# Strided q and k transposes issued one pair step earlier, and the attention of chunk 1 begun with its first layer-1 block

## The chip, the cores and the metric

The kernel runs on one core of one Trainium2 chip. The metric is the device time of one execution in microseconds (us). Engines are named as in the profile: PE (TensorE matmul), PEld (its weight loads), DVE (VectorE), ACT (ScalarE), POOL (GpSimd) and SP (SyncE, which here only issues DMAs).

## The reference, cut to what matters

Sparse attention over 8 batches, 8 heads, 576 positions and head size 64, followed by a two-layer network over the 4608 tokens.

```python
mask_local = (rel >= 0) & (rel < stride)                                    # heads 0-3, stride 32
mask_strided = (rel >= 0) & (pos[None, :] % stride == pos[:, None] % stride)  # heads 4-7
...
attn = exp(masked scores); attn = attn / sum; out = attn @ v
x = attn_out.transpose(0, 2, 1, 3).reshape(B * S, H * D)     # 4608 x 512
h = x @ w_in                                                 # 512 -> 2048
g = np.maximum(h, 0.0) + alpha * np.minimum(h, 0.0)
return g @ w_out                                             # 2048 -> 512
```

## The kernel before, in words

**Chunks.** The network works on nine chunks of 512 tokens. For each chunk, sixteen layer-1 blocks (`lin1_piece`, four matmuls at L636, then a negative part on ACT at L646 and the combination into `gT` on DVE at L649) are followed by layer 2: sixteen pieces of plain matmuls in chunks 0 and 1 (L663), and fourteen blocks of a scheme with sums of quadrants in the later chunks (`lin2_sums`, matmuls at L759, sums at L705).

**Attention between the blocks.** The attention of later batches is cut into small pieces in one list, and after each block of the network some of them run. A pair `g` is two heads of one batch: `g // 4` is the batch, `g % 4` of 0 and 1 are local pairs, 2 and 3 strided ones. The list is made by "pair steps" `g`: in step `g`, the scores of pair `g` (piece S, `score_both`, matmuls L411, exponentials L424 and L430 on ACT, masks L426 and L433 on POOL), the products with v of pair `g - 1` (pieces P, `pv_piece`, L454, then L461 and L463 on DVE), and in some steps the TensorE transposes of a local q and k (pieces T and Tk, L251). A piece also issues loads and casts.

**Order of chunk 1.** The loop from L923 on spreads the pieces of a chunk evenly with an accumulator: `left` pieces over the blocks, half a share per layer-1 block. In chunk 1, `skip = 4` leaves the first four layer-1 blocks without attention and makes the share of the others larger.

**Strided q and k of batches 2 to 7.** `load_d` (L133) loads both into `qks` (names `qsd`, `ksd`) by two DMAs of the POOL queue; for batch c + 1 it is called in step `4c + 2`, for batch 2 ahead of the loop. `transpose_d` (L140) then issues two transposing DMAs from SP, into `qTs[1]` and `kTs[1]`. It is called in the last P piece of step `4c` for batch c. The first reader is the S piece of step `4c + 2` (scores of pairs 10, 14, 18, 22, 26, 30, here called S10 to S30). The last earlier reader of the same tiles is the S piece of step `4c - 1`.

**SP in order.** SP issues, in the order of the program, the stores of the output (L669 and L712), the loads of local q and k (L126), the transposes of attention results (`x_dma`: `xs<-x16s` at L486 for the first strided pair of a batch, `xT<-x` at L488 for local pairs) and `transpose_d`. In step `4c + 3` the last P piece calls `x_dma` for pair `4c + 2`; that is L486. The tile `xs` is read by an ACT copy at L493 (`x_copy`) two steps later.

Of the kernel before, what the change touches and what calls it, by code (L numbers as in the profile page):

```python
# [31 lines left out]
def kernel(  # L32
# [13 lines left out]
    B, H, S, D = q.shape  # L46
# [52 lines left out]
    DX = 2  # L99
# [12 lines left out]
    def load_qk(b, strided, nm):  # L112

        h0 = 4 if strided else 0
        src = q if nm == "q" else k
        if strided and b:
            t16 = hpool.tile([128, 2, 512], F16, tag=f"{nm}s", bufs=2, name=f"{nm}s")
            cast16[(b, True, nm)] = t16  # L120
        else:
            t16 = hpool.tile([128, 2, 512], F32, tag=f"{nm}l", bufs=2, name=f"{nm}l")
            loaded[(b, strided, nm)] = t16
        base = src[b, h0 : h0 + 1, 0:1, :]
        eng = nc.sync if (b > 2 and not strided) or (b == 0 and strided) else nc.gpsimd
        keep(eng.dma_start(t16, bass.AP(  # L126
            tensor=base.tensor, offset=base.offset,
            ap=[[8 * D, 64], [2 * S * D, 2], [S * D, 2], [1, 8 * D]])))
# [7 lines left out]
    def transpose_d():  # L136

        for nm, dst in (("q", qTs[1]), ("k", kTs[1])):
            o = dst.rearrange("r e c -> r (e c)")[:, 0:1280].rearrange("r (j p) -> r j p", p=80)
            keep(nc.sync.dma_start_transpose(o, qks[nm].rearrange("p h c -> p (h c)")))  # L140
# [10 lines left out]
    def cast_l(b, nm, eng="pool"):  # L151
        t16 = hpool.tile([128, 8, 2, 64], F16, tag=f"{nm}l16", bufs=2, name=f"{nm}l16")
        cast_copy(eng, t16, loaded[(b, False, nm)].rearrange("p f (t d) -> p t f d", t=8))
        cast16[(b, False, nm)] = t16

    def load_tail(b, strided):

        t16 = tpool.tile([128, 512], F16, tag="tl", name="tl16")
        for i, src in enumerate((q, k)):
            if strided:  # L160
                keep(nc.gpsimd.dma_start(
                    t16[32 * i : 32 * i + 32, :].rearrange("x (h c) -> x h c", h=4),
                    src[b, 4:8, 512:576, :].rearrange("h (x c) d -> x h (c d)", c=2)))
            else:
                keep(nc.gpsimd.dma_start(
                    t16[64 * i : 64 * i + 64, 0:256].rearrange("p (h d) -> p h d", h=4),
                    src[b, 0:4, 512:576, :].rearrange("h p d -> p h d")))
        cast16[(b, strided, "tail")] = t16

    def load_v(b, strided):  # L170


        if strided:
            st = spool.tile([128, 2048], F16, tag="v", bufs=2, name="stv")
            keep(nc.gpsimd.dma_start(
                st[0:72, :].rearrange("p (h e) -> p h e", h=4),
                v[b, 4:8, :, :].rearrange("h (p t) d -> p h (t d)", t=8)))
            loaded[b] = st
        else:
            v16 = vls[b % 2]  # L180
            base = v[b, 0:1, 0:1, :]
            r0 = 32 if b < 2 else 0
            keep(nc.gpsimd.dma_start(
                v16[r0:128, :, 0:64],
                bass.AP(tensor=base.tensor, offset=base.offset - (32 - r0) * D,
                        ap=[[D, 128 - r0], [96 * D, 24], [1, D]])))
            cast16[(b, False, "v")] = v16
# [9 lines left out]
    def cast_v(b, pr, eng):  # L197

        v16 = vss[b % 2]
        cast_copy(eng, v16[0:72, 2 * pr : 2 * pr + 2, :, 0:64],  # L200
                  loaded[b][0:72, 1024 * pr : 1024 * pr + 1024].rearrange(
                      "p (h t d) -> p h t d", h=2, t=8))
        cast16[(b, True, "v")] = v16
# [300 lines left out]
    def T(u, nm):  # L504
        return lambda: transpose_piece(u, nm)
# [4 lines left out]
    def Pv(g, i):  # L510
        return lambda: pv_piece(pairs[g], i)

    def X(g):
        return lambda: x_piece(pairs[g])
# [27 lines left out]
    for g in range(7, npair + 2):  # L542
        c = g // 4
        a, p, t = g, g - 1, g + 1
        okA = 8 <= a < npair
        okP = 8 <= p < npair
        okT = 8 <= t < npair and (t % 4 == 0 or t < 4 * DX and t % 2 == 0)
        nP = len(pairs[p].pgroups) if okP else 0
        seq = []
        if okA:  # L550
            seq.append(("S", lambda a=a: score_both(pairs[a])))
        if okP:
            seq.append(("P", Pv(p, 0)))
        if okT:
            seq.append(("T", T(t // 2, "q")))
        if 8 <= g - 2 < npair and not pairs[g - 2].xd:
            seq.append(("X", X(g - 2)))
        if okP:
            seq.append(("P", Pv(p, 1)))
        if okT:  # L560
            seq.append(("Tk", T(t // 2, "k")))
        if nP == 3:
            seq.append(("P", Pv(p, 2)))
        if not seq:
            seq.append(("N", lambda: None))

        todo = [(c, pr) for pr in range(2)] if g % 4 == 0 and 8 <= g < npair else []

        if g % 4 == 1 and 9 <= g and c + 1 < B:
            todo = [(c + 1, nm) for nm in "qk"]  # L570
        lastP = max([i for i, z in enumerate(seq) if z[0] == "P"], default=len(seq) - 1)
        nslots = [i for i, z in enumerate(seq) if z[0][0] != "S"] or list(range(len(seq)))
        for i, (kind, fn) in enumerate(seq):
            extra = []
            if todo and i in nslots:
                left = len([z for z in nslots if z >= i])
                cnt = -(-len(todo) // max(1, left))
                extra = [todo.pop(0) for _ in range(min(cnt, len(todo)))]

            def run(fn=fn, extra=extra, g=g, c=c, kind=kind, lastp=(i == lastP), first=(i == 0)):  # L580
                fn()
                for b, pr in extra:
                    if pr in ("q", "k"):
                        cast_l(b, pr)
                        if b + 1 < B:
                            load_qk(b + 1, False, pr)
                        continue
                    cast_v(b, pr, "pool")
                    if pr == 1 and b + 1 < B:
                        load_v(b + 1, True)  # L590
                if kind == "Tk" and g % 4 == 3 and c + 3 < B:
                    load_tail(c + 3, False)
                if lastp:
                    if 4 * DX <= g - 1 < npair and pairs[g - 1].xd:
                        x_dma(pairs[g - 1])
                    if g % 4 == 0 and DX <= c < B:
                        transpose_d()
                    if g % 4 == 2 and DX <= c and c + 1 < B:
                        load_d(c + 1)
                    if g % 4 == 1 and DX < c and c + 1 < B:  # L600
                        load_v(c + 1, False)
                if first and 4 * DX <= g - 3 < npair and pairs[g - 3].xd and pairs[g - 3].strided:
                    x_copy(pairs[g - 3])
            feed(run, g - 2 if kind == "X" else -1)
# [318 lines left out]
    for n in range(1, NCH):  # L923
        ab = attn_until(n + 1) if n + 1 < B else len(pieces)
        left = ab - pos["i"]
        skip = 4 if n == 1 else 0
        acc = 0.0
        for i in range(32 if n == 1 else 30):
            if i < 16:
                if quiet(n):  # L930
                    lin1_piece(n, 8 * (i % 2) + i // 2)
                    if i in (3, 7, 11):
                        late.append(lambda i=i: g_sum(nc.gpsimd, n, 1, i // 2 - 1, i // 2 + 1))
                else:
                    lin1_piece(n, i)
                    if n > 1 and i in (10, 12):
                        g_sum(nc.gpsimd, n, 3, 2 * i - 20, 2 * i - 16)
                    if n > 1 and i == 13:
                        late.append(lambda: g_sum(nc.vector, n, 1, 0, 4))
            elif n == 1:  # L940
                lin2_piece(n, i - 16)
            else:
                lin2_sums(n, i - 16)
                if n == 2 and i == 20:
                    w_sums(nc.vector, (3,))
            if i >= skip:
                acc += left / ((22.5 if n == 1 else 19 if n == B - 2 else 20.5) - 0.5 * skip) * (0.5 if i < 16 else 1.0)
            cnt = int(acc)
            acc -= cnt
            attn_n(cnt, ab)  # L950
        while pos["i"] < ab:
            attn_step(ab)
# [30 lines left out]
```

The softmax here doesn't subtract the row's maximum and nothing guards it: scores larger than these inputs give would overflow.

## Time and profile before

| what | value |
|---|---|
| median of 5 runs | 324.2 us |
| the 5 runs | 323.23, 323.28, 325.19, 324.2, 328.4 us |
| the profiled execution | 323.23 us, of which 321.5 us are the span |
| PE busy | 303.1 us (94% of the span) |
| DVE, ACT, POOL busy | 221.3, 180.7, 171.8 us |
| software DMA queue (q0, from POOL), hardware queue (q1, from SP) | 49.6% and 33.4% of 16 engines' span |

The span runs from the first to the last instruction of the program; 1.7 us of the execution's time lie outside it. Busy shares are averages over stages: layers 1 and 2 of chunks 1 to 5 with attention between them (66 to 232 us) have other limits than the last chunks, in which no attention is left. A wait in the profile is named by the engine that waits, its line, and what released it.

### The profile page before, as it was taken

The numbers are of one execution on the slowest core, as the hardware profiler recorded it, in microseconds if no ns is written. First come the engines' busy times: TensorE is split into PE (matmuls) and PEld (weight loads), VectorE is DVE, ScalarE is ACT, GpSimd is POOL, SyncE is SP. The second block draws the span as 40 slices with busy tenths as digits, with TensorE's granted clock in tenths as the row PEclk, the third lists the DMA queues.
The fourth block names the chain that finished last, engine by engine and source line by source line (L and its number), as shares of the span: only waits on it lengthen the run. The fifth ranks groups of instructions, "written<-read, shape, count | busy, mean of one in ns | idle before, by whom it ended". The sixth has DMA issues, their size and how long they took to land.

```text
span 321.5 us, 7079 instructions
## 1 busy us (share of the span) xinstructions
PE 303.1 (94%) x2813; PEld 194.6 (61%) x2813; DVE 221.3 (69%) x403; ACT 180.7 (56%) x331; POOL 171.8 (53%) x170
## 2 busy tenths in 40 slices
PE   7699989999999999999998999799999999999995
PEld 2365446554454457745787878346864794585484
DVE  5466855766633789578756895578658986865872
ACT  1565655459566666477556745576477527624730
POOL 8672397323999691969195908494536501200300
PEclk9999999999999999999999999999999999999999
DMA  7999999999389991999369935993281122002003
GB/s 217 191 205 206 225 177 167 183 207 240 64 152 144 247 120 9 116 272 155 37 99 226 198 38 97 139 154 45 48 187 20 19 83 70 2 33 100 0 2 132
DMA packets 81057, 40.38 MB, mean 126 GB/s; under 512 B 58480, under 2 KB 76160, under 8 KB 81024
## 3 DMA queue, kind: packets, MB, share of 16 engines
q0 software_dynamic: 41728, 17.38, 49.6%
q1 hardware_dynamic: 39296, 22.55, 33.4%
q8 instruction: 22, 0.36, 0.5%
q14 instruction: 11, 0.09, 0.1%
HBM read 38.01 MB, written 9.44 MB: 148 GB/s over the span
## 4 chain that ended last, share of the span: by engine, by line
PE 63%; DMA 12%; DVE 12%; ACT 6%; issue 3%; POOL 2%; SPq 1%; ACTq 0%
PE hb L636 22%; PE hb L759 21%; DMA kT<-ksd 10%; PE hb L663 7%; DVE gT L649 6%; PE pv L454 3%; DMA kl<-in_k_dram 2%; DVE gsum L705 2%; DVE x L463 2%; ACT neg L646 2%; PE sp L411 2%; PE tp L251 2%; PE hb L817 2%; PE opl L759 1%; ACT et L430 1%
## 5 line engine op out<-in xcount | busy, mean ns | idle before, releaser
L649 DVE SCALAR_TENSOR_TENSOR gT<-neg,oma,hb 128x512 f16<-128x512 f32 x144 | 105.3, 744 | 43.7 <-ACT neg L646 36.7
L636 PE MATMUL hb<-xT,win 128*128 128x512 f16 (+1 forms) x640 | 132.6, 358 | 0.7
L646 ACT ACTIVATE neg<-hb 128x512 f32<-128x512 f32 x144 | 86.1, 598 | 39.1 <-PE hb L636 37.6
L636 PEld LDWEIGHTS <-win 128*128 128x128 f16 x640 | 60.2, 98 | 56.8 <-issue 2.7
L426 POOL TENSOR_TENSOR et<-et,consts 128x576 f16<-128x576 f16 (+1 forms) x24 | 30.6, 1274 | 64.6 <-ACT et L424 64.3
L705 POOL TENSOR_TENSOR gsum<-gT 128x1024 f16<-128x1024 f16 (+1 forms) x16 | 28.0, 1766 | 42.2 <-DVE gT L649 42.2
L759 PEld LDWEIGHTS <-gsum 128*128 128x128 f16 x448 | 41.8, 98 | 5.0
L759 PEld LDWEIGHTS <-gT 128*128 128x128 f16 x336 | 31.4, 98 | 8.4 <-issue 3.4
L463 DVE TENSOR_TENSOR x<-pv,rc 96x384 f16<-96x384 f32 (+2 forms) x62 | 33.0, 532 | 2.1
L663 PE MATMUL hb<-wout,gT 128*128 128x512 f16 x128 | 32.7, 379 | 0.1
L461 DVE RECIPROCAL rc<-pv 72x6 f32<-72x6 f32 (+2 forms) x80 | 14.7, 183 | 25.2 <-PE pv L454 24.9
L433 POOL TENSOR_TENSOR et<-et,consts 128x576 f16<-128x576 f16 (+1 forms) x24 | 30.9, 1288 | 0.9 <-ACT et L430 0.6
L454 PEld LDWEIGHTS <-et 72*128 72x128 f16 (+1 forms) x448 | 24.1, 98 | 10.8 <-POOL et L433 0.9
L759 PE MATMUL hb<-wout,gT 128*128 128x256 f16 x216 | 27.4, 273 | 3.0 <-DVE gT L649 3.0
L771 ACT COPY o<-hb 128x512 f32<-128x512 f32 (+1 forms) x28 | 15.8, 564 | 24.5 <-PE hb L759 24.2
L424 ACT ACTIVATE et<-sp 128x576 f16<-128x576 f32 (+1 forms) x24 | 15.5, 646 | 21.8 <-PE sp L411 21.8
L759 PE MATMUL hb<-wsum,gsum 128*128 128x256 f16 x216 | 26.3, 273 | 0.0
L759 PE MATMUL hb<-wout,gsum 128*128 128x256 f16 x216 | 26.2, 272 | 0.0
L774 DVE TENSOR_TENSOR o<-hb,o 128x512 f32<-128x512 f32 (+1 forms) x21 | 14.2, 678 | 12.7 <-PE hb L759 8.7
L430 ACT ACTIVATE et<-sph 128x288 f16<-128x288 f32 (+1 forms) x48 | 18.5, 407 | 0.0
L817 PE MATMUL hb<-gsum 128*128 128x512 f16 x44 | 16.4, 449 | 1.2 <-DVE gsum L829 1.2
L663 PEld LDWEIGHTS <-gT 128*128 128x128 f16 x128 | 10.7, 97 | 8.7 <-issue 0.2
(107 smaller groups left out, 328.6 us busy)
## 6 DMA issues: line engine op xcount, KB each, us to landing
out_dram<-o SPq DMA_DIRECT2D x27, 256.0 KB, 2.5
ql<-in_q_dram SPq DMA_DIRECT2D x6, 512.0 KB, 5.3
kl<-in_k_dram SPq DMA_DIRECT2D x6, 512.0 KB, 6.6
stv<-in_v_dram POOLq DMA_DIRECT2D x8, 288.0 KB, 7.9
vl<-in_v_dram POOLq DMA_DIRECT2D x6, 384.0 KB, 12.2
win<-in_moe_w_in_dram POOLq DMA_DIRECT2D x4, 512.0 KB, 9.6
wout<-in_moe_w_out_dram POOLq DMA_DIRECT2D x4, 512.0 KB, 13.2
out_dram<-osb SPq DMA_DIRECT2D x8, 256.0 KB, 3.9
```

The costliest lines, as they stand in the source:

```text
L426: keep(nc.gpsimd.tensor_tensor(mv, mv, m, op=ALU.mult))
L430: keep(nc.scalar.activation(ev[:, n * y : n * y + n], sps[y][0:r, 0:n], AF.Exp, scale=SCALE))
L433: keep(nc.gpsimd.tensor_tensor(mv, mv, m, op=ALU.mult))
L454: keep(nc.tensor.matmul(pv[:, 65 * x : 65 * x + 65], et[0:r, c : c + 128], v16[0:r, 2 * P.pr + hh, t, :] if P.strided else v16[:, 6 * (2 * ...
L463: keep(nc.vector.tensor_tensor(P.x16[0:w, c0 : c0 + 64 * nb].rearrange("r (c e) -> r c e", e=64), pvv[:, :, 0:64], rc[0:w, 0:nb].unsqueeze ...
L636: keep(nc.tensor.matmul(hps[:, dst : dst + w], win16[:, kk, 128 * m : 128 * m + 128], xT[:, kk, src : src + w], start=(kk == 0 and x == 0) ...
L646: keep(nc.scalar.activation(neg, hps, AF.Relu, scale=-1.0))
L649: keep(nc.vector.scalar_tensor_tensor(gTs[n][:, m, :], neg, oma[:, m : m + 1], hps, op0=ALU.mult, op1=ALU.add))
L663: keep(nc.tensor.matmul(ops, gTs[n][:, kf, 128 * mt : 128 * mt + 128], wout16[:, kf, :], start=(kf == 0), stop=(kf == 15)))
L705: keep(eng.tensor_tensor(o[:, k0:k1], x[:, k0:k1], y[:, k0:k1], op=op))
L759: keep(nc.tensor.matmul(dst, lhs[:, kf, 128 * mt : 128 * mt + 128], rhs[:, kf, :], start=(first and own and kf == 0), stop=(kf == 7), skip ...
L817: keep(nc.tensor.matmul(wps, wrm[:, 0:128], wrm, start=True, stop=True))
```

## The change

`transpose_d()` is called in the last P piece of step `4c + 3` for batch c + 1, right behind `x_dma`, instead of in step `4c + 4`. For batch 2 it moves from the S piece of step 8 to the Tk piece of step 7. In chunk 1 the accumulator starts with the first layer-1 block, and the divisor is the 22.5 that was there without the skip.

```diff
@@ -593,7 +593,7 @@
                 if lastp:
                     if 4 * DX <= g - 1 < npair and pairs[g - 1].xd:
                         x_dma(pairs[g - 1])
-                    if g % 4 == 0 and DX <= c < B:
+                    if g % 4 == 3 and DX <= c + 1 < B:
                         transpose_d()
                     if g % 4 == 2 and DX <= c and c + 1 < B:
                         load_d(c + 1)
@@ -923,7 +923,6 @@
     for n in range(1, NCH):
         ab = attn_until(n + 1) if n + 1 < B else len(pieces)
         left = ab - pos["i"]
-        skip = 4 if n == 1 else 0
         acc = 0.0
         for i in range(32 if n == 1 else 30):
             if i < 16:
@@ -943,8 +942,7 @@
                 lin2_sums(n, i - 16)
                 if n == 2 and i == 20:
                     w_sums(nc.vector, (3,))
-            if i >= skip:
-                acc += left / ((22.5 if n == 1 else 19 if n == B - 2 else 20.5) - 0.5 * skip) * (0.5 if i < 16 else 1.0)
+            acc += left / (22.5 if n == 1 else 19 if n == B - 2 else 20.5) * (0.5 if i < 16 else 1.0)
             cnt = int(acc)
             acc -= cnt
             attn_n(cnt, ab)
```

## The prediction

> **What bounds the kernel now.** I read the page's slices first, then PE's waits, the timeline at each of those waits, SP's timeline ahead of them, and last the landing times of the transfers. The slices of the page (40 of 8.04 us) show PE nearly full, at full clock:
>
> ```profile
> PE   7699989999999999999998999799999999999995
> PEclk9999999999999999999999999999999999999999
> ```
>
> So a microsecond in which PE stands still is a microsecond of the span, unless another engine takes it back later. PE's two largest waits after the start-up (us in total, times, longest):
>
> ```profile
> PE sp L411 <- DMA kT<-ksd: 3.7, 3, 2.1
> PE hb L759 <- DVE gT L649: 3.0, 4, 0.8
> ```
>
> The first is what the change aims at. The timeline shows where it lies (start, us, instruction; in brackets PE's idle time before it):
>
> ```profile
> 107.47 0.30 PE L411 MATMUL sp<-qT,kT 64*128 64x72 f16 x8 [0.70 <-DMA kT<-ksd]
> ...
> 140.29 0.30 PE L411 MATMUL sp<-qT,kT 64*128 64x72 f16 x8
> ...
> 173.70 0.30 PE L411 MATMUL sp<-qT,kT 64*128 64x72 f16 x8 [0.82 <-DMA kT<-ksd]
> ...
> 208.36 0.30 PE L411 MATMUL sp<-qT,kT 64*128 64x72 f16 x8 [2.13 <-DMA kT<-ksd]
> ```
>
> These are S14, S18, S22 and S26. At 140.29 the PE work before it ended at 140.17 (138.28 + 1.89), so 0.12 us were idle; an S piece that waits for no transfer has no gap (S19 at 148.34, the blocks before it run to 148.41 as modelled). S10 and S30 don't wait. The SP queue ahead of S26:
>
> ```profile
> 192.68 1.20 SPq L486 DMA_TRANSPOSE xs<-x16s  x1
> 196.83 0.38 SPq L712 DMA_DIRECT2D out_dram<-o  x1
> 197.31 1.31 SPq L140 DMA_TRANSPOSE qT<-qsd  x1
> 198.72 2.13 SPq L140 DMA_TRANSPOSE kT<-ksd  x1
> ```
>
> The transposes stand behind a store that waits for layer 2. How long they then take differs; from issue to landing (last column), first for this pair, then for the last batch's, issued at 231.91 and 233.34, where no more v is loaded beside them:
>
> ```profile
> qT<-qsd SPq DMA_TRANSPOSE x1, 7.6
> kT<-ksd SPq DMA_TRANSPOSE x1, 9.6
> ```
>
> ```profile
> qT<-qsd SPq DMA_TRANSPOSE x1, 3.8
> kT<-ksd SPq DMA_TRANSPOSE x1, 4.3
> ```
>
> The DMA engines are idle just ahead of the old place (columns: stretch, its us, busy of PE, PEld, DVE, ACT, POOL, clock, DMA share, GB/s; xs is issued at 127.56, the old transposes at 131.27):
>
> ```profile
> 124.00:128.00 4.00, 3.96 (x52) 3.15 (x51) 3.47 (x7) 2.62 (x6) 0.63 (x1) 1.00 0.00 0
> ...
> 132.00:136.00 4.00, 3.85 (x51) 3.10 (x44) 1.90 (x4) 3.39 (x6) 3.69 (x4) 1.00 1.07 148
> ```
>
> **The move of the transposes.** Nothing is added or taken out: six calls of two DMAs each, as before. On SP they pass the store of step 4c + 4 (L712, or L669 in chunk 1) and nothing else; on POOL they pass nothing, but the v load of that step (L175, issued at 131.79, 164.64, 198.04) is now issued behind them. They stand directly behind xs (L486), which itself waits for DVE's x16s, so the gain in issue time is far less than a pair step (32.7 / 4 = 8 us). Old to new issue of kT, taking xs's issue, its 1.2 to 1.34 us, 0.1, and the 1.4 from qT to kT: batch 3 99.99 to 96.6, batch 4 132.68 to 130.3, batch 5 165.78 to 162.0, batch 6 198.72 to 195.4: 2.4 to 3.8 us earlier.
>
> How long they take there the trace doesn't show. The ends: 4.3 us, the pair without a v load, and 9.6, the slowest. Even at 9.6 they land at 106.2, 139.9, 171.6 and 205.0, and PE wants them at 106.77, 140.17, 172.88 and 206.23. I take about 5, since the engines are idle then and the v load comes behind. Later batches shift as a whole, issue and need together, so the margins stay.
>
> The waits that this adds: in step 4c + 3 the transposes need the loads of `load_d`. For batches 4 to 7 these are issued at 111 to 213 and take 9 to 10 us, so are there 4 us or more before xs is. For batch 3 it is close (below). The readers of the old contents, S11, S15 and so on, ran 10 us earlier. Queued behind the transposes on SP are stores, 2 to 3.7 us later; an output tile has its next writer in the next chunk, after sixteen layer-1 blocks of 0.87 us, so they cost nothing; without that cover each would cost its 2 to 3 us. Ahead is xs, whose reader is ACT's copy L493 at 132.71, 5 us after the issue.
>
> What of the idle time comes back: the steps from S14 to S18, S22 and S26 take 32.82, 33.41 and 34.66 us. Without the idle time at their ends these are 32.70, 32.59 and 32.53: the rest hardly depends on how long PE stood. Three new steps then take 97.82 instead of 100.89, 3.07 less, and at S14 0.70 goes: 3.77 in all. The rest that follows a longer wait is the shorter by a tenth, so 0.1 to 0.4 may return as DVE, in those stretches the next busiest, has less time to catch up, its gT being what layer 2 waits for next (0.8, four times). I take 3.5.
>
> **The start of chunk 1.** There are 22 pieces. Old shares: 22 / 20.5 / 2 = 0.537 from block 4 on; new: 22 / 22.5 / 2 = 0.489 from block 0. The first piece comes after block 2 instead of 5, S8 after 6 instead of 9, S10 after 14 instead of 16, and from block 23 on old and new agree. The same matmuls, in another mix: PE cost nothing. PE idles 0.43 us in all from 66.5 to 99.0, so at most 0.4 is to be won; as much may be lost if a P piece meets its mask too early, as one does now (0.4 at 82.97). The spacing S8 to P(8,1), six blocks, is the same, so I take 0. What it moves is POOL:
>
> ```profile
> 77.61 1.27 POOL L426 TENSOR_TENSOR et<-et,consts 128x576 f16<-128x576 f16 x1 [11.10 <-ACT et L424]
> ...
> 89.74 0.78 POOL L133 DMA_DIRECT2D qsd<-in_q_dram  x1
> 90.51 0.71 POOL L133 DMA_DIRECT2D ksd<-in_k_dram  x1
> ```
>
> POOL is busy without a gap between these, so with S8 three blocks (2.6 us) earlier the loads of batch 3 go out near 87.1 and 87.9. They took 5.2 and 6.5 us and would be there at 92.3 and 94.4, ahead of xs's end at 95.1. Without this edit they land at 97.0, and kT would go out near 98.5, landing at 105.9 if it takes its old 7.4. So this edit pays for S14's 0.70 at most, and is hidden otherwise.
>
> **A rule against it.** The trace has kT landing 7.4 to 9.6 us after issue. The Trainium skill, DMA: Bandwidth & Descriptors, sections Anatomy of one DMA and Latency and other measured facts, gives about 2 us fixed and 261 GB/s for a transpose with non-contiguous middle dimension. For 80 x 2048 values of 2 bytes (328 KB) that is my estimate of 3.3 us. By it kT of batch 6 would land at 202.0 even in the old place, 4 us before it is wanted, and moving it would gain 0. The pair without a v load (4.3) is near the rule, the others are twice as slow, and PE demonstrably starts at their landing. The measurement decides: 3.5, not 0.
>
> **The sum.** 323.23 - 3.5 = 319.7 for the profiled execution. The median of the runs stands 1.0 above that execution (324.2), so 320.7 for the median.
>
> **The rivals.** (1) Forecast: all four waits go, 2.8 to 4.1 us; chance 0.68, 320.1 to 321.4. (2) Partly: xs, in the same hardware queue, took 5.5 us to land in chunk 1 and 4.1 in the next, not the 2.7 of later ones; if the transposes queue up behind it and lengthen past 10 us, the waits at S22 and S26 shrink by their 3 us of earlier issue at most, less what is lost. Gain 1.7 to 2.5, 321.7 to 322.5; chance 0.12. Against it: idle engines at 124 to 128. (3) The time comes back: PE arrives earlier at the first layer-2 blocks and waits there for DVE's gT instead, four times 0.6 more. Then 3.5 - 2.4 = 1.1 is left, or somewhat less, 323.1 to 323.7; for it, DVE is busy 3.8 to 3.9 of 4 us at 112 to 124; against it, the equal rests of the three steps. Chance 0.11. (4) Slower: xs lands later because 650 KB of transposes now follow it at once. ACT's copy L493 stands in order before the deferred exponentials (133.92) and the evictions of layer 1 (136.57). It decides from the point at which xs lands after 132.7; layer 1 turns over three banks of 0.87 us, so PE lets ACT be about 1.7 us late for free (two blocks). Were xs to land with kT (about 136.5), ACT would be 3.8 late, PE 2 per batch, five batches 10, less the 3.5: 330.7; at half of the 10, 325.7. Against it: xs is first in its queue. Chance 0.09, slower.
>
> **How the numbers follow.** A measurement of this kernel can tell about 0.5% (1.6 us) from no change. Faster: cases 1 and 2, 0.80; same: case 3, 0.11; slower: case 4, 0.09. The range 319.2 to 324.0 takes in cases 1 to 3, the 0.4 of chunk 1 either way, and about 0.5 of scatter of a median below; left out are case 4 and the tails.
>
> **What would show it.** In the profile after: no wait of L411 for kT, S14 to S26 spaced 32.6 to 32.8 us; SP with L486 and then both L140, the store behind; kT landing 4 to 6 us after issue; load_d of batch 3 near 87. Case 2 keeps a wait at S26; case 3 a wait at L759 grown beyond 0.8; case 4 an ACT wait at L493 for xs. I am wrong if PE's idle time before those four S pieces stays, or if it goes and the span doesn't shrink by 2 us.

## The result, and the profile after

The changed kernel takes 0.9883 of the time before (95% interval 0.9862 to 0.9904), that is 1.2% or 3.8 us less. Medians: 321.59 us against 324.2. The prediction was 320.7 us with a gain of 3.5. Some executions of both kernels run slower than the others, at a lower granted clock; the ratio compares the faster ones alone, while the medians, 2.6 us apart, take in all.

| | before | after |
|---|---|---|
| span of the profiled execution | 321.5 us | 316.6 us |
| start of chunk 1 (first L636 of it) | 66.48 | 65.45 |
| S12 | 93.96 | 92.81 |
| S12 to the end of the span | 227.54 | 223.79 |
| S13 to S14 | 9.09 | 8.33 |
| S14 to S18, S18 to S22, S22 to S26, S26 to S30 | 32.82, 33.41, 34.66, 34.40 | 32.74, 32.60, 32.55, 34.50 |

The two spans differ by 4.9 us, more than the runs do. 1.0 of it lies ahead of chunk 1, where nothing was changed, and that stretch varies from execution to execution: over all profiles here chunk 1 starts anywhere from 64.9 to 72.8 us. I therefore compare profiles from S12 to the end of the span, and leave totals to the ratios. From S12 the gain is 3.75 us; from the first block of chunk 1 to S12, where the second edit acts, it is 0.12 (27.48 to 27.36).

The slices of the page, PE and its clock, after:

```profile
PE   6999989999999998999899989998999999999995
PEclk9999998999999999999999999999999999999999
```

PE's waits: none of L411 for a transfer is left, and the one for gT is little larger than the 3.0 us of before.

```profile
PE hb L759 <- DVE gT L649: 3.4, 4, 0.9
```

The same four S pieces in PE's timeline, now without a bracket (no idle time ahead of them):

```profile
105.55 0.30 PE L411 MATMUL sp<-qT,kT 64*128 64x72 f16 x8
...
138.29 0.30 PE L411 MATMUL sp<-qT,kT 64*128 64x72 f16 x8
...
170.89 0.30 PE L411 MATMUL sp<-qT,kT 64*128 64x72 f16 x8
...
203.44 0.30 PE L411 MATMUL sp<-qT,kT 64*128 64x72 f16 x8
```

The SP queue ahead of S26: xs, both transposes behind it, the stores last.

```profile
189.95 1.20 SPq L486 DMA_TRANSPOSE xs<-x16s  x1
191.26 1.35 SPq L140 DMA_TRANSPOSE qT<-qsd  x1
192.70 1.95 SPq L140 DMA_TRANSPOSE kT<-ksd  x1
194.74 5.29 SPq L712 DMA_DIRECT2D out_dram<-o  x4
```

From issue to landing (last column), kT of this pair (S26) first, then kT of S18, issued at 129.42:

```profile
kT<-ksd SPq DMA_TRANSPOSE x1, 4.4
```

```profile
kT<-ksd SPq DMA_TRANSPOSE x1, 7.3
```

kT of S26 lands at 197.1, 6 us early. kT of S18 lands at 136.7 and is wanted at about 138.2: 1.5 us to spare. The DMA engines now work from 124 to 128 us, a stretch that was empty before (DMA share 0.61).

POOL issues the loads of batch 3 here:

```profile
86.11 0.78 POOL L133 DMA_DIRECT2D qsd<-in_q_dram  x1
86.89 0.71 POOL L133 DMA_DIRECT2D ksd<-in_k_dram  x1
```

They are issued 20.7 us after the start of chunk 1 instead of 23.3.

### The profile page after: what moved, and what is told of

It reads as the page before. It is cut to its first block, busy times and chain, and to the rows that moved or that the text cites. A ratio compares the mean times of both kernels' runs of the same rounds, so it can differ in the third digit from the quotient of the medians.

```text
span 316.6 us, 7079 instructions
## 1 busy us (share of the span) xinstructions
PE 303.5 (96%) x2813; PEld 195.4 (62%) x2813; DVE 222.0 (70%) x403; ACT 180.1 (57%) x331; POOL 171.7 (54%) x170
## 4 chain that ended last, share of the span: by engine, by line
PE 71%; DVE 12%; ACT 9%; issue 3%; POOL 2%; DMA 1%; SPq 0%; ACTq 0%
PE hb L636 26%; PE hb L759 22%; PE hb L663 8%; DVE gT L649 6%; PE pv L454 3%; DVE gsum L705 2%; PE tp L251 2%; ACT xT L493 2%; DVE x L463 2%; ACT neg L646 2%; PE hb L817 2%; ACT et L430 2%; ACT et L424 2%; PE sp L411 2%; PE xp L471 1%
## 5 line engine op out<-in xcount | busy, mean ns | idle before, releaser
L636 PE MATMUL hb<-xT,win 128*128 128x512 f16 (+1 forms) x640 | 132.9, 358 | 0.7
L649 DVE SCALAR_TENSOR_TENSOR gT<-neg,oma,hb 128x512 f16<-128x512 f32 x144 | 105.3, 744 | 40.0 <-ACT neg L646 33.2
L636 PEld LDWEIGHTS <-win 128*128 128x128 f16 x640 | 60.1, 98 | 56.3 <-issue 2.7
L426 POOL TENSOR_TENSOR et<-et,consts 128x576 f16<-128x576 f16 (+1 forms) x24 | 30.6, 1273 | 61.2 <-ACT et L424 61.1
L705 POOL TENSOR_TENSOR gsum<-gT 128x1024 f16<-128x1024 f16 (+1 forms) x16 | 28.0, 1766 | 42.2 <-DVE gT L649 42.2
L759 PEld LDWEIGHTS <-gsum 128*128 128x128 f16 x448 | 41.8, 98 | 5.0
L759 PEld LDWEIGHTS <-gT 128*128 128x128 f16 x336 | 31.4, 98 | 8.7 <-issue 3.8
L663 PE MATMUL hb<-wout,gT 128*128 128x512 f16 x128 | 33.6, 387 | 0.0
L759 PE MATMUL hb<-wout,gT 128*128 128x256 f16 x216 | 27.4, 273 | 3.4 <-DVE gT L649 3.4
L759 PE MATMUL hb<-wsum,gsum 128*128 128x256 f16 x216 | 26.3, 273 | 0.0
L759 PE MATMUL hb<-wout,gsum 128*128 128x256 f16 x216 | 26.2, 272 | 0.0
L817 PE MATMUL hb<-gsum 128*128 128x512 f16 x44 | 15.7, 430 | 1.2 <-DVE gsum L829 1.2
```

The lines of the kernel that those rows point to most:

```text
L426: keep(nc.gpsimd.tensor_tensor(mv, mv, m, op=ALU.mult))
L636: keep(nc.tensor.matmul(hps[:, dst : dst + w], win16[:, kk, 128 * m : 128 * m + 128], xT[:, kk, src : src + w], start=(kk == 0 and x == 0) ...
L649: keep(nc.vector.scalar_tensor_tensor(gTs[n][:, m, :], neg, oma[:, m : m + 1], hps, op0=ALU.mult, op1=ALU.add))
L663: keep(nc.tensor.matmul(ops, gTs[n][:, kf, 128 * mt : 128 * mt + 128], wout16[:, kf, :], start=(kf == 0), stop=(kf == 15)))
L705: keep(eng.tensor_tensor(o[:, k0:k1], x[:, k0:k1], y[:, k0:k1], op=op))
L759: keep(nc.tensor.matmul(dst, lhs[:, kf, 128 * mt : 128 * mt + 128], rhs[:, kf, :], start=(first and own and kf == 0), stop=(kf == 7), skip ...
```

## The experiments

Theory A, as the expectations below call it: PE's idle time ahead of S14, S18, S22 and S26 is paid in full (a microsecond of waiting is a microsecond of the run), and the transposes are late because they stand behind a store and share the DMA engines with the load of the strided v (L175, "the v load"). Rivals: the gain comes from the new start of chunk 1; the time comes back in layer 2; being behind xs matters. All ratios are to the kernel before, from runs beside it.

**One half of the change each.** First the transposes alone:

```diff
-                    if g % 4 == 0 and DX <= c < B:
+                    if g % 4 == 3 and DX <= c + 1 < B:
                         transpose_d()
```

> The transposes in step 4c+3, the start of chunk 1 as before (four blocks without attention). Theory A (PE's idle time at S14, S18, S22, S26 is paid in full, and it is the move of the transposes that takes it away): all four waits go, 3.4 to 3.8 us less than before, ratio 0.988 to 0.990; batch 3's kT goes out near 98, held back by the load of batch 3 that lands at 97, and lands with 0 to 1 us to spare. Theory B (the earlier start of chunk 1 brings a good part): only S18 to S26 gain, 3.0 us or less, and the wait at S14 stays at 0.5 us or more.

Measured 0.9904 (0.9871 to 0.9937); S12 to the end 224.81 us, 1.0 more than with both edits. The wait at S14 is gone: kT of batch 3, issued at 100.48, landed after 4.7 us, which left 3.9 us to spare and not the 0 to 1 expected. S13 to S14 takes 8.65 us, 0.3 more than with both edits, as xs took 5.9 us to land there, ACT waited 0.21 us for it, and PE at L471 0.49 us for ACT (0.16 with both edits). One wait for kT is left elsewhere (PE's timeline):

```profile
142.55 0.30 PE L411 MATMUL sp<-qT,kT 64*128 64x72 f16 x8 [0.67 <-DMA kT<-ksd]
```

That is S18: kT was issued at 133.39 and took 9.1 us. So the move carries nearly all of the gain (the two intervals overlap widely), and the pair of batch 4 is the one with little margin. Then the start of chunk 1 alone, the other two parts of the diff:

> The transposes in their old place, attention of chunk 1 from its first layer-1 block. Theory A: the waits stay as before (0.7, 0.1, 0.8, 2.1 us), the time is that of before within 0.5 us, ratio 0.998 to 1.002. Theory B: 1 us or more less, ratio below 0.997.

Measured 1.0116 (1.0050 to 1.0182), which neither theory expected. Its profile has the waits as before (0.82, none, 0.61, 1.61) and 226.83 us from S12 to the end, 0.7 less than the kernel before; but S12 starts at 100.07. The same kernel once more:

> The start of chunk 1 alone, again: its first run came out 1.2% slower with six timed runs, while its profile from S12 on is 0.7 us shorter than that of the kernel before and all its loss lies in the first 66 us, where the program is the same. If that loss is the start-up's scatter, ratio 0.997 to 1.003 now; if the edit itself costs, 1.006 or more again, and the loss must then be found between 66 us and S12.

Measured 1.0023 (0.9968 to 1.0077), with 228.02 us from S12 (waits 1.26, 0.16, 0.85, 2.02) and S12 at 94.98. The two intervals overlap only between 1.0050 and 1.0077. The loss did not repeat. In the first profile it lies ahead of the edit: chunk 1 starts at 72.70 us instead of 66.48, with a clock of 0.75 from 15 to 30 us. Where the edit acts, from the first block of chunk 1 to S12, both profiles take 27.37 us, the kernel before 27.48. So the edit alone changes 0.1 us there; by the ratios alone a cost of up to 0.8% would not be excluded.

**What makes the transposes slow.** The kernel before, the v load moved out of their way, first into the step of `load_d`:

```diff
-                    if pr == 1 and b + 1 < B:
-                        load_v(b + 1, True)
...
                         load_d(c + 1)
+                        load_v(c + 1, True)
```

> The kernel before, with the load of the strided v of batch c+1 (L175) issued in step 4c+2 behind load_d instead of in step 4c+4; the transposes stay in their old place. If it is this load that slows them (theory A's second half: 7.0 to 9.6 us with it beside them, 3.8 and 4.3 without), kT of batches 4 to 6 lands 4 to 5 us after its issue, the waits at S18, S22 and S26 go without any move of the transposes, about 3 us less than before, ratio near 0.991; S14 may keep its 0.7. If the slow landing comes from what else runs there (stores of the output, loads of local q and k), landing stays at 7 us or more and the time is that of before.

Measured 1.0008 (0.9956 to 1.0061). Half of it came as theory A has it: no S piece waits, and kT of batches 4 to 6 lands 4.5, 4.3 and 6.4 us after issue. The idle time ahead of S18, S22 and S26, 3.1 us before, is gone. But two new waits take it back (L648, L704 and L758 here are L649, L705 and L759; the first two rows are PE's waits, then follow the timelines of ACT, and of DVE and POOL):

```profile
PE hb L758 <- DVE gT L648: 6.2, 4, 1.6
PE xp L471 <- ACT et L430: 2.6, 2, 2.5
```

```profile
102.60 1.30 ACT L493 COPY xT<-xs 128x576 f16<-128x576 f16 x1 [2.20 <-DMA xs<-x16s]
```

```profile
122.43 2.46 DVE L704 TENSOR_TENSOR gsum<-gT 128x1024 f16<-128x1024 f16 x1
123.08 1.26 POOL L433 TENSOR_TENSOR et<-et,consts 72x576 f16<-72x576 f16 x1
```

The same two in the kernel before, and the next sum of the same size, which has no mask beside it:

```profile
118.09 1.26 POOL L433 TENSOR_TENSOR et<-et,consts 72x576 f16<-72x576 f16 x1
118.25 1.66 DVE L705 TENSOR_TENSOR gsum<-gT 128x1024 f16<-128x1024 f16 x1
...
121.95 0.69 DVE L705 TENSOR_TENSOR gsum<-gT 128x1024 f16<-128x1024 f16 x1
```

In chunk 1 the v load runs beside xs, which lands after 7.8 us; ACT waits for it, PE waits 2.47 us for ACT and then runs at a clock of 0.50 (105.5 to 107.5 us): 3.2 us more from S13 to S14. In chunks 2 to 5 the issue of the v load (0.7 us on POOL) shifts POOL's masks, and the first quadrant sum on DVE, 1.66 us before, takes 2.46: 0.8 us in each of four chunks. The sum now starts beside the mask ahead of the one shown (L426, 121.84 to 123.11) and ends behind both. In both kernels that sum ends 0.55 us after the last POOL mask that runs beside it (119.91 and 119.35; 124.89 and 124.34), while the same instruction takes 0.69 beside no mask. That fits the rule of the Trainium skill, SBUF — State Buffer, section Who interferes with whom: a two-input DVE operation on SBUF and a POOL operation that reads it exclude each other. 3.2 + 3.2 - 3.1 = 3.3 us; S12 to the end shows 3.1 more (230.66 against 227.54). The ratio allows 2.0 us more at most, so this profile has somewhat more of the loss than the executions that the ratio compares; that the gain is lost, both show.

So the load was moved again, where neither happens:

```diff
-                    if pr == 1 and b + 1 < B:
+                    if pr == 1 and b in (2, 3):
                         load_v(b + 1, True)
...
+                if kind == "Tk" and g % 4 == 3 and DX < c < B - 2:
+                    load_v(c + 2, True)
```

> The kernel before, transposes and start of chunk 1 in their old places; only the loads of the strided v of batches 5, 6 and 7 are issued in step 4c+3 of batches 3 to 5, behind the tail loads (POOL, some 10 us before the transposes of step 4c+4), so that neither the transposes nor POOL's quadrant sums have them beside or ahead of them. Theory A (the v load doubles the transposes' time; PE's wait is paid in full): kT of batches 4 to 6 lands 4 to 6 us after its issue, the waits at S18, S22 and S26 go (S14 keeps 0.7), nothing else grows, 3 us less than before, ratio 0.989 to 0.993. Rival (the time saved at these waits is taken back by DVE in layer 2, as the earlier attempt with the v load seemed to show): ratio 0.997 or more, with L759 waiting for gT longer than 0.8 each.

Measured 0.9906 (0.9867 to 0.9945), 224.46 us from S12. Only S14 waits, and the pair of S26 lands 3.9 (qT) and 6.2 us (kT) after issue in its old place:

```profile
PE sp L411 <- DMA kT<-ksd: 0.5, 1, 0.5
```

```profile
kT<-ksd SPq DMA_TRANSPOSE x1, 6.2
```

S14 to S18, S22 and S26 take 32.64, 32.61 and 32.54 us, as after the change, with the transposes where they were. The transposes were late for two reasons, their place on SP and the v load beside them. At S22 and S26 taking away either is enough. At S18 taking away the load is; the earlier place alone is not always: of the five profiles with the transposes right behind xs, two keep a wait there (0.67 and 0.29 us). What exactly the load and the transposes share, the DMA engines or something on the way to them, these runs do not separate.

**Is the wait paid one for one?** The opposite step, a longer wait: the kernel before with the transposes called in the first piece of step 4c + 1:

```diff
-                    if g % 4 == 0 and DX <= c < B:
-                        transpose_d()
...
+                if first and g % 4 == 1 and DX <= c < B:
+                    transpose_d()
```

> The kernel before, with the transposes of batches 4 to 7 one piece later: on SP they stand behind one more store and go out about 1.9 us later (batch 3 is not moved). Theory A, one for one: the waits at S18, S22 and S26 grow by 1.9 each to about 2.0, 2.7 and 4.0 us, 5 to 6 us more than before, ratio 1.015 to 1.018. Rival (a longer wait lets DVE and ACT catch up and is given back in the rest of the step): the waits grow as much but the steps from S to S less, 2 to 3 us more, ratio 1.006 to 1.010.

Measured 1.0357 (1.0257 to 1.0457), twice theory A's number. The waits grew about as forecast (0.44, 2.02, 2.88, 2.95, together 8.3 against 3.8), and from S12 the profile is 7.8 us longer, not 4.5. What is missing follows the two longest waits. S22 in PE's timeline, and the stretches behind it (clock third from the right):

```profile
179.96 0.31 PE L411 MATMUL sp<-qT,kT 64*128 64x72 f16 x8 [2.88 <-DMA kT<-ksd]
```

```profile
180.00:182.00 2.00, 2.00 (x24) 1.47 (x25) 0.00 (x0) 0.94 (x2) 0.90 (x1) 0.53 1.44 308
182.00:184.00 2.00, 2.00 (x13) 1.51 (x12) 0.75 (x1) 0.99 (x3) 0.97 (x2) 0.61 1.04 398
```

And the kernel before, behind its longest wait, of 2.13 us:

```profile
208.30:210.30 2.00, 1.94 (x24) 1.06 (x25) 0.00 (x0) 1.45 (x4) 0.81 (x1) 1.00 1.36 296
```

After 2.88 us of standing still PE runs some 4 us at a clock near half, after 2.13 at full clock. S22 to S23 and S26 to S27 take 9.68 and 9.63 us here and 8.07 and 8.04 before: 1.6 more twice. 4.5 + 3.2 = 7.7 of 7.8 us. Nothing is given back. The ratio says more, some 11.6 us (8.3 to 14.8); the profiled execution, the fastest of the six, is 10.2 us longer than that of before, 2.4 of it ahead of S12. What the others lose beyond it has no trace and stays open.

**Does the place behind xs matter?** The changed kernel with the transposes ahead of xs:

```diff
+                    if g % 4 == 3 and DX <= c + 1 < B:
+                        transpose_d()
                     if 4 * DX <= g - 1 < npair and pairs[g - 1].xd:
                         x_dma(pairs[g - 1])
-                    if g % 4 == 3 and DX <= c + 1 < B:
-                        transpose_d()
```

> The changed kernel with the two transposes of step 4c+3 ahead of xs on SP, so that they don't wait for DVE's x16s and go out as soon as the loads of load_d are there, about 4 to 6 us earlier still. If being behind xs costs nothing (theory A), the time is that of the changed kernel within 0.5 us (ratio to the kernel before 0.987 to 0.990), no S piece waits. Rival 4 of the prediction (xs landing later because of the transposes, ACT held at L493): then xs, now alone behind them, is waited for less or more, and the time differs from the changed kernel's by 1 us or more.

Measured 1.0020 (0.9981 to 1.0059): the whole gain is gone. In the profile it goes at one place, chunk 1 (SP's, ACT's and PE's timelines):

```profile
100.44 1.59 SPq L140 DMA_TRANSPOSE qT<-qsd  x1
102.73 1.50 SPq L140 DMA_TRANSPOSE kT<-ksd  x1
104.32 2.03 SPq L486 DMA_TRANSPOSE xs<-x16s  x1
```

```profile
108.91 1.30 ACT L493 COPY xT<-xs 128x576 f16<-128x576 f16 x1 [3.27 <-DMA xs<-x16s]
```

```profile
110.57 0.42 PE L471 MATMUL xp<-consts,x 72*128 72x72 f16 x8 [3.54 <-ACT et L430]
```

In this chunk the transposes go out no earlier than xs did, 0.3 us after S12. Their issue, with 0.6 us of waiting for the load of ksd, holds SP for 3.9 us, and xs goes out behind them. ACT's copy waits for xs with the exponentials behind, and PE then waits for ACT. S13 to S14 takes 13.39 us instead of 8.33, 3.5 for the wait and the rest under a clock of 0.77 (109 to 113 us) and 0.60 (113 to 115) around and after it. In the later chunks kT goes out some 7 us ahead of xs, which costs nothing and gains nothing (32.74, 32.61, 32.54).

**A version that beats both.** The largest wait that is left is L759 for gT: ahead of it DVE makes a quadrant sum between two gT. DVE's timeline, after:

```profile
116.33 1.77 DVE L705 TENSOR_TENSOR gsum<-gT 128x1024 f16<-128x1024 f16 x1
...
118.71 1.39 DVE L649 SCALAR_TENSOR_TENSOR gT<-neg,oma,hb 128x512 f16<-128x512 f32 x2
```

```diff
-                    if n > 1 and i == 13:
-                        late.append(lambda: g_sum(nc.vector, n, 1, 0, 4))
...
-                g_sum(nc.vector, n, 1, 4, 8)
+                g_sum(nc.vector, n, 1, 0, 8)
```

> The changed kernel with one more change: the first quadrant sum on DVE (L705, 1.7 us) no longer stands between the gT of blocks 13 and 14; it is made in one instruction (about 1.2 us) at the beginning of layer 2, behind the last gT. The next largest wait of PE after the transposes, L759 for gT, 0.8 us in each of chunks 2 to 5, 3.4 us in all. If PE's idle time is paid one for one, 2.5 to 3.4 us less than the changed kernel, ratio to the kernel before 0.978 to 0.982. If the sums are then late for the matmuls of wsum, the wait only moves there and the gain is under 1 us.

Measured 0.9754 (0.9696 to 0.9812); 220.41 us from S12, 3.38 less than the changed kernel. The sum is made in one instruction, beside no mask of POOL, and PE's four waits for gT are gone; the largest left at L759 is small:

```profile
120.13 1.23 DVE L705 TENSOR_TENSOR gsum<-gT 128x2048 f16<-128x2048 f16 x1
```

```profile
PE hb L759 <- DVE gsum L705: 0.4, 1, 0.4
```

The same version once more, and then the changed kernel again beside the runs of its first time:

> The changed kernel with the first quadrant sum behind the last gT, again, for a narrower interval: ratio to the kernel before 0.974 to 0.980.

Measured 0.9764 (0.9705 to 0.9822), median 315.66 us; 220.38 us from S12.

> The changed kernel again, on the same chip and beside the same runs of the kernel before as the other three: ratio 0.986 to 0.990.

Measured 0.9894 (0.9824 to 0.9965); 224.12 us from S12, with a wait of 0.29 us at S18. Against this, the version with the sum behind the last gT is 1.4% faster (0.9754 / 0.9894 = 0.986; the intervals of the two do not overlap), and 1.1% of the span by the profiles (3.4 us). PE's wait went with the sum's place; how much of the gain comes from the one instruction that replaced two was not tried apart.

## Why the prediction was right, point by point

- **The four waits go.** Right: 3.7 us of L411 waiting became none. The steps were to be 32.6 to 32.8 us; they are 32.74, 32.60 and 32.55, which is the old rest (32.70, 32.59, 32.53) to within 0.04.
- **The issue.** kT was to go out about 2.8 us after xs: 2.76 and 2.75 for S22 and S26. It was 3.28 for S14 and 3.67 for S18, as qT's issue there took 1.83 and 2.27 us instead of 1.3. (The loads of `load_d` for batch 7 took 5.0 and 6.5 us before, not the 9 to 10 that the prediction gives for batches 4 to 7; nothing hung on it.)
- **The landing, about 5 us.** Right for S14, S22 and S26 (5.4, 4.5, 4.4), wrong for S18: 7.3, 9.1 with the transposes alone; the move did not make this pair faster than its old 7.6. The argument was that the engines are idle there and the v load comes behind. For S18 it comes only 0.6 us behind kT (129.98 against 129.42), with the transposes alone 0.1; for S14, S22 and S26 it is 2.0 to 2.6. The prediction's bound of 9.6 us left 0.3 us at this place, and two runs used it up: waits of 0.67 and 0.29. That S18 did not wait in the profile of the changed kernel is in part luck. xs takes 4.0 us at S14 and S18 and 2.6 to 2.7 later; why is open.
- **0.3 us given back to DVE.** Too cautious. The steps grew over the old ones without their idle time by 0.04, 0.01, 0.02 and, for S26 to S30, 0.10. The longer wait showed no return either, and more than full price.
- **Start of chunk 1 at 0.** Right in size: from its first block to S12 chunk 1 takes 27.36 us instead of 27.48. POOL's loads moved by 2.6 us as worked out. It was to pay at S14 at most: S13 to S14 takes 8.33 with it, 8.65 without. But that 0.3 is no wait for kT, which had 3.9 us to spare without the edit; it is ACT's wait for xs.
- **The rule against.** The traces decide for the v load: the pair of S26 in its old place lands after 9.6 us with it beside and 6.2 without, those of S18 and S22 after 7.6 and 7.9 with it and 4.5 without, and the time follows. The prediction took its 2 us from a section on DMAs issued from GpSimd, while the transposes go out from SP; the 3.8 and 4.3 us of an undisturbed pair are the better guide here.
- **The rivals.** The time did not come back in layer 2. The rival of xs landing late did not happen in the changed kernel, and with the transposes alone it cost 0.3 us. With xs put behind the transposes it cost 5 us in the profile (0.0126 or 4.1 us by the ratios 1.0020 and 0.9894), all at one place, where the prediction had priced 2 per batch over five batches.
- **The sum.** 3.5 predicted, 3.75 from S12 in the profile, 3.8 by the ratio. The 0.25 between is the return to DVE that did not come. The median came out at 321.59 instead of 320.7.

## What to carry to other kernels

When the bound engine waits for a transfer, read its landing time beside that of a twin with less traffic: issuing earlier and taking the traffic away were worth the same 1% here, and which is simpler is the choice. Before moving a transfer past others on an in-order queue, ask what its reader holds up: here the transfer whose reader came first, with the most work queued behind that reader, had to stay first. Ask too what the moved transfer itself still waits for, as everything behind it on the queue waits with it. A load moved away from one wait can lengthen two others; account for each step of the timeline until the sum matches the total.

## What the runs showed of the hardware

- PE's granted clock fell to between 0.50 and 0.77 (means of 2 to 4 us) after waits of 2.47, 2.88, 2.95 and 3.54 us and stayed at 1.00 after 2.13 and 2.02; between 66 and 262 us it fell nowhere else in the twelve profiles. In the two cases measured directly (S22 and S26 above) a fall cost about 1.6 us more. The Trainium skill, TensorE: Matmul & The Clock Gate, What's actually happening, gives an idle window of about 3.4 us; here waits from 2.47 us on were enough. A wait of this length thus cost more than its own time.
- A DVE sum of 128x1024 took 0.69 us beside no mask of POOL, and 1.66, 1.77 and 2.46 beside one, ending 0.55 us after the mask each time. A 128x2048 one took 1.23 beside no mask, less than the half-sized one beside a mask.
